# A small expert's rider on TensorE: partial sums kept in each column group, one transpose for each, and a written order

## The chip, the cores and the metric

One Trainium2 chip, one core. The metric is the device time of one execution in microseconds (us); of several executions the median is given. Instructions run on TensorE (PE, its weight loads listed apart as PEld), VectorE (DVE), ScalarE (ACT), GpSimd (POOL), and DMA queues that SyncE (SP) issues. Each engine has an instruction queue of its own.

## The reference

Three layers in a row, all in float32: attention with a learned relative bias, a mixture of experts, and a feed-forward layer. The change is in the second.

```python
x = attn_out.transpose(0, 2, 1, 3).reshape(1152, 512)
# mixture of experts: E = 8 experts, D = 512, F = 1024, capacity 288
logits = x @ w_gate
expert_idx = np.argmax(logits, axis=1)
gate_w = softmax(logits)[row, expert_idx]
# the first 288 rows of each expert, in order, are kept
h = np.maximum(np.einsum('ecd,edf->ecf', disp, w1), 0.0)
y = np.einsum('ecf,efd->ecd', h, w2)
out[i] = gate_w[i] * y[expert_idx[i], pos[i]]     # 0 for a row that is not kept
# feed-forward, 512 -> 2048 -> 512
h = x @ w_in
g = np.maximum(h, 0.0) + alpha * np.minimum(h, 0.0)
return g @ w_out
```

## The kernel before

Attention runs first. Routing then sorts the kept rows by expert into a table in DRAM, and the experts that got rows are worked off one after the other, each with its rows turned so that features lie on partitions. Matrices of the experts and of the last layer are split into a high and a low part (names ending in `h` and `l`), and each product is the sum of three products of parts. The course that runs in the traces (`J.mode == 1`) has a first expert of up to 288 rows (`job`, on `J.x`), a second one of up to 288 rows (`group(g1, ...)`, which calls `job` again), and a third one with at most 32 rows (`TINY`). Then `ffn(0, 608)` computes the last layer on the 608 rows of the table and sends each row to its place.

`job` goes over `f` = 0 to 7, slices of 128 of the expert's 1024 hidden units. `layer1(f)` (L690) is 12 matmuls of 128x128 weights on 288 columns into the tile `g`; ACT writes `hh = relu(g)`, DVE `hl`. `layer2(f - 1)` (L705) is 12 more into `acc`. The weights of two `f` come as one quarter of the expert (`raw`), which `raw_split` turns into `w1h, w1l, w2h, w2l` on ACT (L602) and DVE (L603). `side(2 * f)` is called between `layer1(f)` and `layer2(f - 1)`, `side(2 * f + 1)` behind the latter: at these 16 steps other work can be put in.

The third expert is such work, the **rider**. It holds few rows, so its weights are not split, and it computes in plain float32, which TensorE does in two passes for a matmul. The rows are the stationary operand (128x32), the weights stream, and four matmuls go to four groups of 32 columns of the array at once: matmul `c` writes partitions `32c` to `32c + 31` of the PSUM tile. `rider` gives back a `begin`, which loads the rows and the first matrix in quarters, and a list of steps; `RT` holds the number of the step at which each is called:

- `transpose` (L794): the 32 rows are turned to `x`, 4 chunks of 128 features (`xrT`, copied by DVE to `m`).
- `partial(q)` (L801), `q` = 0 to 3, a quarter of 256 hidden units each: the four column groups hold the four chunks of the contraction, 256 columns each; ACT copies the tile `part` to a `cell`.
- `hidden(q)` (L808): two matmuls with `fold`, a matrix of stacked identities, add the four chunks and turn the result, tile `hT`; ACT applies relu (L809) into `R.h`.
- `layer2(q)` (L818): the four column groups hold two chunks of the contraction by two halves of the 512 outputs, 256 columns each, added over `q` in `racc`.
- `finish`: ACT copies `racc`, two more matmuls with `fold` (`yT`, L826) add and turn, ACT and DVE write `yh` and `yl`, the input of the last layer.
- `load2(q)` (L777) loads a quarter of the second matrix over the quarter of the first one that `partial(q)` has read.

The parts of the first matrix lie in `AH["more"]` (named `ah` in the trace), in two halves of the quarter `raw` that `g1` has used up, and in two tiles `xj`.

Beside the rider the steps call `ahead(i)`, which converts the first 64-bit weights of the last layer (`d`, `cv`, `cw`; L860 on ACT, L862 to L864 on DVE). In the last layer `weights(f)` does the same for the other slices, from three buffers `d` that SP fills.

The part of the kernel up to the end of the first expert is under a manual schedule: on PE, ACT and DVE instructions stand in the order of the code. From `two_groups` on, a scheduler with a model of the costs orders each engine's instructions, SP's DMA issues too.

Of the kernel before, what the change touches and what calls it, by code (L numbers as in the profile page):

```python
# [15 lines left out]
AF = mybir.ActivationFunctionType  # L16
ALU = mybir.AluOpType
AX = mybir.AxisListType
ET = mybir.EngineType
# [13 lines left out]
BIG = float(1 << 20)  # L33
PRE0 = 10
NB = 2
RT = (0, 1, 2, 3, 4, 5, 6, 7, 9, 11, 12)
Q3 = 1
PRE = 4

# [1 line left out]
def build(tc, nc, a):  # L41
    V, A, G, T, SY = nc.vector, nc.scalar, nc.gpsimd, nc.tensor, nc.sync
    with contextlib.ExitStack() as ctx:
# [712 lines left out]
        def rider(g, e, yo):  # L756


            n = TINY
            w1, w2 = [a[z][ds(e, 1)].rearrange("a x y -> (a x) y") for z in ("ew1", "ew2")]  # L760
            x, xr = g.few[:, :, 0:n], g.ts[0][:n]
            R, S = Unit(), {}

            def cell():
                return M.p.tile([128, 512], F32, tag="cw", name="cell", bufs=4)

            def cells(q, n):

                t = [(AH["more"], *g1.t)[q]] if q < 3 else g.ts[1:]
                z = [z.rearrange("p (k c) -> p k c", c=n) for z in t]  # L770
                S[q] = [x[:, j] for x in z for j in range(x.shape[1])]
                return z

            def load(q, w, n):
                z = cells(q, n)
                for x, y in zip(z, (w,) if len(z) == 1 else (w[:, 0:512 // n], w[:, 512 // n:])):
                    SY.dma_start(x, y)  # L777

            def load1(q):
                load(q, w1[:, 256 * q:256 * q + 256].rearrange("(k p) c -> p k c", p=128), 256)  # L780

            def load2(q):
                load(q, w2[256 * q:256 * q + 256, :].rearrange("(f p) n -> p f n", p=128), 512)

            def begin():
                rows_of.other(SY.dma_start(xr, xd[ds(yo, n), 0:DM]))
                for q in range(4):
                    load1(q)

            def transpose():  # L790
                R.h = cell()
                ps = ps1(pt, "xrT")[:, 0:4 * n].rearrange("p (k n) -> p k n", k=4)
                for k in range(4):
                    T.transpose(ps[:, k], xr[:, 128 * k:128 * k + 128], ident[:n, :n])  # L794
                V.tensor_copy(x, ps)

            def partial(q):
                w = S[q]
                ps = ps1(pt, "part")[:, 0:256]
                for k in range(4):  # L800
                    T.matmul(ps[n * k:n * k + n], x[:, k], w[k], start=True, stop=True, skip_group_check=True)  # L801
                R.p = cell()[:, 0:256]
                A.copy(R.p, ps)

            def hidden(q):
                ps = ps1(pt, "hT")[:, 0:2 * n]
                for j in range(2):
                    T.matmul(ps[:, n * j:n * j + n], R.p[:, 128 * j:128 * j + 128], fold[:, 2 * n:3 * n], start=True, stop=True)  # L808
                A.activation(R.h[:, 2 * n * q:2 * n * q + 2 * n], ps, AF.Relu)  # L809

            def layer2(q):
                if q == 0:
                    R.acc = ps1(pt, "racc")[:, 0:256]
                w = S[q]
                for j in range(2):
                    for d in range(2):
                        o = n * (2 * j + d)
                        T.matmul(R.acc[o:o + n], R.h[:, n * (2 * q + j):][:, 0:n], w[j][:, 256 * d:256 * d + 256],  # L818
                                 start=q == 0, stop=q == 3, skip_group_check=True)

            def finish():
                y = cell()[:, 0:256]
                A.copy(y, R.acc)
                ps = ps1(pt, "yT")[:, 0:4 * n].rearrange("p (c r) -> p c r", c=2)
                for c in range(2):
                    T.matmul(ps[:, c], y[:, 128 * c:128 * c + 128], fold[:, 0:2 * n], start=True, stop=True)  # L826

                ps = ps.rearrange("p c (d r) -> p d c r", d=2)
                yh, yl = [z.rearrange("p (d c) r -> p d c r", d=2)[:, :, :, ds(yo, n)] for z in (M.yh, M.yl)]
                A.copy(yh, ps)  # L830
                V.tensor_tensor(yl, ps, yh.bitcast(F32), ALU.subtract)

            return begin, [(i, lambda f=f, q=q: f(*q)) for i, f, *q in (
                (RT[0], transpose), (RT[1], partial, 0), (RT[1], load2, 0),
                (RT[2], hidden, 0), (RT[2], partial, 1), (RT[2], load2, 1), (RT[3], hidden, 1), (RT[3], partial, 2), (RT[3], load2, 2),
                (RT[4], hidden, 2), (RT[4], partial, 3), (RT[4], load2, 3), (RT[5], hidden, 3), (RT[6], layer2, 0),
                (RT[7], layer2, 1), (RT[8], layer2, 2), (RT[9], layer2, 3), (RT[10], finish))]

        def to_dense(acc, yo, n):
            for d in range(2):  # L840
# [438 lines left out]

        def two_groups(g2, *more):  # L1280
            begin, todo = rider(g2, expert_of(2), row_of(2, [ET.SP, ET.Activation, ET.DVE]))
            group(g1, False, stepper(*more, *todo), begin)

        with tc.If(J.mode == 1) as course:  # L1284
            two_groups(prepare(2, 0), *[(2 * i + 1, lambda i=i: ahead(i)) for i in range(1, PRE)])
# [108 lines left out]
```

## Time and profile before

| | us |
|---|---|
| median of 3 executions | 357.55 |
| lowest, highest | 356.72, 361.35 |
| the profiled execution, its own time | 359.0 |
| span of the profile of that execution | 357.3 |
| PE busy in the span | 339.5 |
| second expert with the rider, first matmul to first matmul of the last layer | 35.55 |

The span runs from the first to the last instruction that the profiler saw; the execution's own time is 1.7 us longer, which lies around it. A row of the timeline is a run of like instructions on one engine: start, time from the first one's start to the last one's end, and what they write and read. Matmuls overlap on TensorE, so the time that a run takes up is read from its start to the start of the next row, not from its duration.

### The profile page before, as it was taken

How to read it: one execution, taken by the hardware profiler on the slowest of the kernel's cores; microseconds unless marked ns; L12 is line 12 of the kernel's file. 1: busy time of each engine (PE TensorE's matmuls, PEld its weight loads, DVE VectorE, ACT ScalarE, POOL GpSimd, SP SyncE). 2: the span in 40 equal slices, each digit the busy share in tenths (PEclk: the TensorE clock that was granted, in tenths of full speed). 3: DMA queues.
4: the chain of work that ended last, by engine and by line, in shares of the span. 5: the costliest groups of instructions: out<-in, count | busy, mean ns of one | idle time of the engine just before them, and what ended most of it. 6: DMA issues, size and time to landing. Idle time of an engine off the chain costs nothing. (4 is left out here: it accounts for less than half of the span.)

```text
span 357.3 us, 8970 instructions
## 1 busy us (share of the span) xinstructions
PE 339.5 (95%) x3372; PEld 273.2 (76%) x3373; DVE 278.7 (78%) x674; ACT 236.4 (66%) x585; POOL 58.8 (16%) x90
## 2 busy tenths in 40 slices
PE   4898999999999999999999999999999999999991
PEld 2334566677899788888899997799988988987880
DVE  4999989977788867876798795369999999988430
ACT  6959899987667675766774473357776656656430
POOL 2055333300000010462262100100000000000023
PEclk9999999999999999999999999999999999999997
DMA  7788969898999853948736996743546645530003
GB/s 301 223 257 273 333 244 354 313 285 313 339 411 337 276 206 108 332 154 258 222 71 189 361 288 187 246 150 125 178 119 189 190 152 178 175 120 3 0 29 118
DMA packets 42048, 76.90 MB, mean 215 GB/s; under 512 B 5159, under 2 KB 19623, under 8 KB 41996
## 3 DMA queue, kind: packets, MB, share of 16 engines
q1 hardware_dynamic: 40812, 73.76, 63.0%
q0 software_dynamic: 1184, 2.48, 1.9%
q8 instruction: 28, 0.46, 0.6%
q14 instruction: 24, 0.20, 0.2%
HBM read 57.53 MB, written 20.09 MB: 217 GB/s over the span
## 5 line engine op out<-in xcount | busy, mean ns | idle before, releaser
L273 ACT ACTIVATE p<-p,mn 128x576 f32<-128x576 f32 x72 | 55.6, 779 | 11.4 <-DVE mn L266 11.2
L259 PE MATMUL sps<-kqv 64*128 64x288 f32 x256 | 61.3, 427 | 0.3 <-DVE mn L266 0.2
L266 DVE CUSTOM_DVE_ANT_0 p<-sps,bias 128x576 f32<-128x576 f32 x72 | 52.4, 751 | 6.2 <-PE sps L252 3.6
L305 PE MATMUL t<-ident,p 64*128 64x64 f32 x640 | 52.6, 227 | 0.6 <-DVE PT L282 0.2
L183 DVE TENSOR_SCALAR h<-c 128x512 f32<-128x512 f32 (+17 forms) x121 | 49.5, 474 | 0.5 <-PE bps L192 0.4
L305 PEld LDWEIGHTS t<-ident,p 64*128 64x128 f32 x640 | 45.3, 139 | 6.0 <-ACT st L200 2.6
L280 ACT COPY PT<-t 128x320 f32<-128x320 f32 (+1 forms) x85 | 30.0, 404 | 24.7 <-PE sps L259 18.6
L259 PEld LDWEIGHTS sps<-kqv 64*128 64x128 f32 x256 | 37.2, 187 | 8.0 <-issue 4.1
L192 PE MATMUL bps<-h,c 128*32 128x512 f32 (+17 forms) x352 | 34.4, 489 | 8.0 <-DVE h L183 5.3
L323 PE MATMUL av<-PT,kqv 128*64 128x128 f32 x512 | 35.3, 279 | 0.8 <-ACT PT L280 0.3
L323 PEld LDWEIGHTS av<-PT,kqv 128*64 128x64 f32 x512 | 27.5, 137 | 8.6 <-ACT PT L280 4.1
L860 ACT ACTIVATE cv<-d 128x512 f32<-128x512 f32 x32 | 21.6, 676 | 14.8 <-DMA d<-in_win 5.5
L200 ACT ACTIVATE st<-bps,c 128x527 f32<-128x527 f32 (+35 forms) x72 | 30.6, 506 | 0.2 <-PE bps L192 0.2
L953 PE MATMUL facc<-w2h,hl 128*128 128x512 f32 (+1 forms) x75 | 29.9, 399 | 0.2 <-DVE hl L603 0.2
L953 PE MATMUL facc<-w2h,hh 128*128 128x512 f32 (+1 forms) x75 | 29.7, 396 | 0.0
L953 PE MATMUL facc<-w2l,hh 128*128 128x512 f32 (+1 forms) x75 | 29.6, 395 | 0.0
L192 PEld LDWEIGHTS bps<-h,c 128*32 128x32 f32 x352 | 10.6, 113 | 23.8 <-issue 7.4
L179 POOL TENSOR_SCALAR h<-c 128x448 f32<-128x448 f32 (+11 forms) x12 | 21.6, 1798 | 36.2 <-PE bps L192 19.5
L941 PE MATMUL fg<-yh,w1l 128*128 128x304 f32 x120 | 26.6, 303 | 0.0
L941 PE MATMUL fg<-yl,w1h 128*128 128x304 f32 x120 | 26.5, 302 | 0.0
L941 PE MATMUL fg<-yh,w1h 128*128 128x304 f32 x120 | 26.5, 302 | 0.0
L282 DVE COPY PT<-t 128x320 f32<-128x320 f32 (+1 forms) x43 | 18.8, 461 | 9.0 <-PE t L305 8.0
(232 smaller groups left out, 691.2 us busy)
## 6 DMA issues: line engine op xcount, KB each, us to landing
bias<-bd SPq DMA_DIRECT2D x23, 576.0 KB, 6.8
bd<-st SPq DMA_DIRECT2D x36, 295.5 KB, 6.7
raw<-in_ew SPq DMA_DIRECT2D x20, 512.0 KB, 6.5
d<-in_win SPq DMA_DIRECT2D x16, 512.0 KB, 3.8
d<-in_wout SPq DMA_DIRECT2D x16, 512.0 KB, 3.9
kqv<-in_kqva SPq DMA_DIRECT2D x6, 736.0 KB, 7.0
kqv<-in_kqvb SPq DMA_DIRECT2D x6, 672.0 KB, 9.3
xd<-zr SPq DMA_DIRECT2D x4, 722.8 KB, 8.6
```

The source lines that it names most:

```text
L179: G.tensor_scalar(h, tab[:, :n], psi[:, i:i + 1], 0.0, ALU.add, ALU.max)
L183: V.tensor_scalar(h, tab[:, :n], psi[:, i:i + 1], 0.0, ALU.add, ALU.max)
L192: T.matmul(ps[32 * c:32 * c + 32, n0:n1], w2n, hs[c][:, n0:n1], start=True, stop=True)
L200: A.activation(st[:, o:o + src.shape[1]], src, AF.Copy, scale=rr[:, t:t + 1])
L259: return [lambda n=n: T.matmul(ps[:, n, :288], q[u.ul][p], k[p, 288 * n:288 * n + 288], start=True, stop=True) for n in range(2)]
L266: V.tensor_tensor_reduce(out.rearrange("p (a b) -> p a b", a=2), ps[:, :, :288], bias.rearrange("p (a b) -> p a b", a=2), -0.125, 3.0e38, ...
L273: A.activation(out, out, AF.Exp, bias=mn, scale=-1.0, accum_out=acc)
L280: A.copy(o, i)
L305: return [lambda i=i, x=x: T.transpose(src[:, i], x[p], ident[p, p]) for i, x in enumerate(rows)], out
L323: T.matmul(o[p, c], u.v[:, j, p], rhs(h, j), start=j == 0, stop=False, skip_group_check=True)
L941: T.matmul(ps, w[:, 128 * k:128 * k + 128], x[:, k, s], start=k + i == 0, stop=k + i == 5)
L953: T.matmul(acc[i][:m], h[:, r:r + m], w, start=f == 0 and j == 0, stop=f == NF - 1 and j == 2)
```

## The change

`partial` now adds over the contraction: for a pair of quarters (`q` and `q + 1`) column group `c` holds 128 hidden units, and its four matmuls over `k` accumulate, so `part` is finished when it leaves PSUM and ACT applies relu at once. `hidden` turns it with one transpose. `layer2` and `finish` do the same with 128 outputs in each column group and the contraction over `f`. Called for `q` = 0 and 2 alone, that makes two `partial`, two `hidden`, two `layer2`. `RT` puts them at later steps, and TensorE is under the manual schedule within `group`.

```diff
-RT = (0, 1, 2, 3, 4, 5, 6, 7, 9, 11, 12)
+RT = (5, 8, 9, 10, 13, 14, 15)
...
             def partial(q):
-                w = S[q]
-                ps = ps1(pt, "part")[:, 0:256]
+                ps = ps1(pt, "part")[:, 0:128]
                 for k in range(4):
-                    T.matmul(ps[n * k:n * k + n], x[:, k], w[k], start=True, stop=True, skip_group_check=True)
-                R.p = cell()[:, 0:256]
-                A.copy(R.p, ps)
+                    for c in range(4):
+                        T.matmul(ps[n * c:n * c + n], x[:, k], S[q + c // 2][k][:, 128 * (c % 2):][:, 0:128], start=k == 0, stop=k == 3,
+                                 skip_group_check=True)
+                R.p = cell()[:, 0:128]
+                A.activation(R.p, ps, AF.Relu)
 
             def hidden(q):
-                ps = ps1(pt, "hT")[:, 0:2 * n]
-                for j in range(2):
-                    T.matmul(ps[:, n * j:n * j + n], R.p[:, 128 * j:128 * j + 128], fold[:, 2 * n:3 * n], start=True, stop=True)
-                A.activation(R.h[:, 2 * n * q:2 * n * q + 2 * n], ps, AF.Relu)
+                ps = ps1(pt, "hT")[:, 0:128]
+                T.transpose(ps, R.p, ident)
+                A.copy(R.h[:, 64 * q:64 * q + 128], ps)
 
             def layer2(q):
...
-                for j in range(2):
-                    for d in range(2):
-                        o = n * (2 * j + d)
-                        T.matmul(R.acc[o:o + n], R.h[:, n * (2 * q + j):][:, 0:n], w[j][:, 256 * d:256 * d + 256],
-                                 start=q == 0, stop=q == 3, skip_group_check=True)
+                for f in range(2 * q, 2 * q + 4):
+                    for c in range(4):
+                        T.matmul(R.acc[n * c:n * c + n], R.h[:, n * f:n * f + n], S[f // 2][f % 2][:, 128 * c:128 * c + 128],
+                                 start=f == 0, stop=f == 7, skip_group_check=True)
 
             def finish():
...
-                ps = ps1(pt, "yT")[:, 0:4 * n].rearrange("p (c r) -> p c r", c=2)
-                for c in range(2):
-                    T.matmul(ps[:, c], y[:, 128 * c:128 * c + 128], fold[:, 0:2 * n], start=True, stop=True)
...
+                ps = ps1(pt, "yT")[:, 0:128]
+                T.transpose(ps, y, ident)
...
-                (RT[0], transpose), (RT[1], partial, 0), (RT[1], load2, 0),
-                (RT[2], hidden, 0), (RT[2], partial, 1), (RT[2], load2, 1), (RT[3], hidden, 1), (RT[3], partial, 2), (RT[3], load2, 2),
-                (RT[4], hidden, 2), (RT[4], partial, 3), (RT[4], load2, 3), (RT[5], hidden, 3), (RT[6], layer2, 0),
-                (RT[7], layer2, 1), (RT[8], layer2, 2), (RT[9], layer2, 3), (RT[10], finish))]
+                (RT[1], partial, 0), (RT[1], load2, 0), (RT[1], load2, 1),
+                (RT[2], hidden, 0), (RT[2], partial, 2), (RT[2], load2, 2), (RT[2], load2, 3), (RT[3], hidden, 2),
+                (RT[4], layer2, 0), (RT[5], layer2, 2), (RT[6], finish))]
...
-            group(g1, False, stepper(*more, *todo), begin)
+            with tc.manual_schedule(engines={ET.PE}):
+                group(g1, False, stepper(*more, *todo), begin)
```

Line numbers behind the rider are four lower in the changed kernel (`fg` is L937 there, `facc` L949), and its `layer2` matmuls are L816.

On PE, around the rider's second layer, there stood before (a matmul's row names output tile, operands, output shape and count):

```order
L705 MATMUL acc<-hl,w2h 128x288
L818 MATMUL racc<-ah_3437,cell 32x256 x4
L705 MATMUL acc<-hl,w2h 128x288 x3
L690 MATMUL g_3893<-xh,w1h 128x288 x4
L690 MATMUL g_3893<-xl,w1h 128x288
L818 MATMUL racc<-raw_3393,cell 32x256 x4
L690 MATMUL g_3893<-xl,w1h 128x288 x3
L690 MATMUL g_3893<-xh,w1l 128x288 x4
L705 MATMUL acc<-hh,w2h 128x288
L818 MATMUL racc<-raw_3393,cell 32x256 x4
L705 MATMUL acc<-hh,w2h 128x288 x3
```

On PE at the same place of the changed kernel, behind `layer1(6)`:

```order
L690 MATMUL g_3911<-xh,w1l 128x288 x4
L705 MATMUL acc<-hh,w2h 128x288 x4
L705 MATMUL acc<-hh,w2l 128x288 x4
L705 MATMUL acc<-hl,w2h 128x288 x4
L816 MATMUL racc<-ah_3437,cell 32x128 x8
L816 MATMUL racc<-raw_3393,cell 32x128 x8
L690 MATMUL g_3957<-xh,w1h 128x288 x4
L690 MATMUL g_3957<-xl,w1h 128x288 x4
L690 MATMUL g_3957<-xh,w1l 128x288 x4
L816 MATMUL racc<-raw_3393,cell 32x128 x8
L816 MATMUL racc<-xj,cell 32x128 x8
L705 MATMUL acc<-hh,w2h 128x288 x4
```

The rider's matmuls, which stood in small groups within the runs of the second expert, now stand in groups of 16 between whole layers.

On DVE, from the start of the second expert, there stood before (`w1l` behind L603 is the low half of the second quarter's first matrix, L862 and L863 belong to `ahead`):

```order
L603 TENSOR_TENSOR w2l<-raw_3393,w2h 128x1024
L694 SCALAR_TENSOR_TENSOR hl<-g_3648,hh 128x288
L862 TENSOR_SCALAR ah_3437<-cv 128x512
L863 SCALAR_TENSOR_TENSOR ah_3437<-cv,ah_3437 128x512
L603 TENSOR_TENSOR w1l<-raw,w1h 128x1024
L694 SCALAR_TENSOR_TENSOR hl<-g_3688,hh 128x288
```

On DVE at the same place of the changed kernel:

```order
L603 TENSOR_TENSOR w2l<-raw_3393,w2h 128x1024
L694 SCALAR_TENSOR_TENSOR hl<-g_3650,hh 128x288
L858 TENSOR_SCALAR cw<-cv 128x512
L858 TENSOR_SCALAR ah_3437<-cv 128x512
L859 SCALAR_TENSOR_TENSOR cw<-cv,cw 128x512
L603 TENSOR_TENSOR w1l<-raw,w1h 128x1024
L694 SCALAR_TENSOR_TENSOR hl<-g_3675,hh 128x288
```

One more conversion (L858) now stands ahead of `w1l`. On SP the two DMAs of the expert's last quarter (L613, L615), which stood between the third and the fourth `load2`, now stand ahead of the first. On ACT the first conversion of the last layer's own weights (`cv<-d`, L856) has moved from behind `layer1(7)`'s `hh` and the rider's `yh` to between the rider's copy of `racc` and its `yh`.

## Rows read from the trace of the kernel before

**Rows 1.** The page: busy time, share of the span and instructions of TensorE.

```profile
PE 339.5 (95%) x3372; PEld 273.2 (76%) x3373; DVE 278.7 (78%) x674; ACT 236.4 (66%) x585; POOL 58.8 (16%) x90
```

**Rows 2.** Windows: stretch, its length, each engine's busy time, PE clock, DMA share, GB/s.

```profile
245.00:255.00 10.00, 10.00 (x57) 8.84 (x56) 10.00 (x21) 7.63 (x18) 0.00 (x0) 1.00 0.56 167
...
315.00:325.00 10.00, 9.77 (x51) 7.63 (x50) 8.41 (x17) 6.09 (x14) 0.00 (x0) 1.00 0.17 58
```

**Rows 3.** Timeline of PE: second expert's start, its third layer1, the last layer's start.

```profile
203.30 0.68 PE L690 MATMUL g<-xh,w1h 128*128 128x288 f32 x4
...
208.61 0.68 PE L690 MATMUL g<-xl,w1h 128*128 128x288 f32 x4
209.19 0.79 PE L690 MATMUL g<-xh,w1l 128*128 128x288 f32 x4
209.82 0.69 PE L705 MATMUL acc<-hh,w2h 128*128 128x288 f32 x4
...
238.85 1.39 PE L941 MATMUL fg<-yh,ah 128*128 128x304 f32 x8
```

**Rows 4.** Timeline of PE: the rider's first `partial` and `hidden` between matmuls of `acc`.

```profile
213.55 0.68 PE L705 MATMUL acc<-hh,w2h 128*128 128x288 f32 x4
214.16 0.64 PE L801 MATMUL part<-ah,m 128*32 128x256 f32 x8
214.73 0.79 PE L705 MATMUL acc<-hh,w2l 128*128 128x288 f32 x4
215.36 0.57 PE L808 MATMUL hT<-fold,cell 128*128 128x32 f32 x4
215.76 0.65 PE L705 MATMUL acc<-hl,w2h 128*128 128x288 f32 x3
216.34 0.64 PE L801 MATMUL part<-raw,m 128*32 128x256 f32 x8
```

**Rows 5.** Timeline of PE: the rider's `transpose`, and half of its last `layer2`.

```profile
211.93 0.29 PE L690 MATMUL g<-xl,w1h 128*128 128x288 f32 x1
212.15 0.43 PE L794 MATMUL xrT<-ident,xj 32*128 32x32 f32 x4
212.51 0.67 PE L690 MATMUL g<-xl,w1h 128*128 128x288 f32 x3
...
230.92 0.63 PE L818 MATMUL racc<-xj,cell 128*32 128x256 f32 x4
231.48 0.67 PE L690 MATMUL g<-xh,w1l 128*128 128x288 f32 x3
```

**Rows 6.** Timeline of PE in attention: a chain of accumulation in two column groups.

```profile
60.87 1.09 PE L323 MATMUL av<-PT,kqv 128*64 128x128 f32 x16
61.80 0.39 PE L325 MATMUL av<-PT,vd 128*64 128x128 f32 x4
```

**Rows 7.** Timeline of PE in routing: four column groups with 128 columns each.

```profile
168.90 0.43 PE L393 MATMUL lgT<-xT,c 128*32 128x128 f32 x8
169.26 1.30 PE L323 MATMUL av<-PT,kqv 128*64 128x128 f32 x15
```

**Rows 8.** Timeline of DVE at the start of the second expert.

```profile
206.85 0.42 DVE L862 TENSOR_SCALAR ah<-cv 128x512 int32<-128x512 int32 x1
207.30 0.69 DVE L863 SCALAR_TENSOR_TENSOR ah<-cv,ah 128x512 int32<-128x512 int32 x1
207.91 1.22 DVE L603 TENSOR_TENSOR w1l<-raw,w1h 128x1024 fp32r<-128x1024 f32 x1
```

**Rows 9.** ACT's and SP's timelines, and the DMAs of L777 from 198 to 262 us.

```profile
227.40 1.05 ACT L602 CAST w1h<-raw 128x1024 fp32r<-128x1024 f32 x1 [0.29 <-DMA raw<-in_ew]
...
219.81 0.37 SPq L613 DMA_DIRECT2D raw<-in_ew  x1
...
228.79 0.38 SPq L849 DMA_DIRECT2D d<-in_win  x1
...
DMA to landing us min/median/max: 3.6/6.8/8.4
```

More of the change, by code (lines that the diff above doesn't have):

```diff
@@ L811, in layer2 @@
+                A.copy(R.h[:, 64 * q:64 * q + 128], ps)
             def layer2(q):
                 if q == 0:
-                    R.acc = ps1(pt, "racc")[:, 0:256]
-                w = S[q]
-                for j in range(2):
-                    for d in range(2):
-                        o = n * (2 * j + d)
-                        T.matmul(R.acc[o:o + n], R.h[:, n * (2 * q + j):][:, 0:n], w[j][:, 256 * d:256 * d + 256],
-                                 start=q == 0, stop=q == 3, skip_group_check=True)
+                    R.acc = ps1(pt, "racc")[:, 0:128]
@@ L821, in finish @@
+                for f in range(2 * q, 2 * q + 4):
+                    for c in range(4):
+                        T.matmul(R.acc[n * c:n * c + n], R.h[:, n * f:n * f + n], S[f // 2][f % 2][:, 128 * c:128 * c + 128],
+                                 start=f == 0, stop=f == 7, skip_group_check=True)
             def finish():
-                y = cell()[:, 0:256]
+                y = cell()[:, 0:128]
                 A.copy(y, R.acc)
-                ps = ps1(pt, "yT")[:, 0:4 * n].rearrange("p (c r) -> p c r", c=2)
@@ L825, in finish @@
-                for c in range(2):
-                    T.matmul(ps[:, c], y[:, 128 * c:128 * c + 128], fold[:, 0:2 * n], start=True, stop=True)
-                ps = ps.rearrange("p c (d r) -> p d c r", d=2)
-                yh, yl = [z.rearrange("p (d c) r -> p d c r", d=2)[:, :, :, ds(yo, n)] for z in (M.yh, M.yl)]
+                ps = ps1(pt, "yT")[:, 0:128]
+                T.transpose(ps, y, ident)
+                ps = ps.rearrange("p (c r) -> p c r", c=4)
+                yh, yl = [z[:, :, ds(yo, n)] for z in (M.yh, M.yl)]
@@ L833, in rider @@
             return begin, [(i, lambda f=f, q=q: f(*q)) for i, f, *q in (
-                (RT[0], transpose), (RT[1], partial, 0), (RT[1], load2, 0),
-                (RT[2], hidden, 0), (RT[2], partial, 1), (RT[2], load2, 1), (RT[3], hidden, 1), (RT[3], partial, 2), (RT[3], load2, 2),
-                (RT[4], hidden, 2), (RT[4], partial, 3), (RT[4], load2, 3), (RT[5], hidden, 3), (RT[6], layer2, 0),
-                (RT[7], layer2, 1), (RT[8], layer2, 2), (RT[9], layer2, 3), (RT[10], finish))]
+                (RT[0], transpose), (RT[1], partial, 0), (RT[1], load2, 0), (RT[1], load2, 1),
+                (RT[2], hidden, 0), (RT[2], partial, 2), (RT[2], load2, 2), (RT[2], load2, 3), (RT[3], hidden, 2),
+                (RT[4], layer2, 0), (RT[5], layer2, 2), (RT[6], finish))]
         def to_dense(acc, yo, n):
```

## Prediction, made before the changed kernel was run

> **What bounds the kernel now.** I read the page's busy times first: TensorE is busy for 339.5 of 357.3 us [rows 1]. A share over the whole span says little about one stage, so the windows came next, over the second expert and the last layer: TensorE is busy for all of 245 to 255 us, at the full granted clock (1.00, the level of 2.4 GHz), and even in the worst stretch of the last layer, 315 to 325 us, for 9.77 of 10 us [rows 2]. So from 203 us to the end one thing sets the pace: the line of matmuls. A matmul taken out of it should bring the end forward by what it held of that line, if the other engines keep up. The timeline of PE, row by row, tells how much the rider holds.
>
> From the second expert's first matmul to the first one of the last layer are 35.55 us (at 203.30, 238.85) [rows 3]. The expert itself has 192 matmuls, 48 runs of four. The first ten runs take 203.30 to 208.61, 0.531 us each, so 48 take 25.5 us. 10.05 us are left. Of these 0.15 are a wait at 209 us, where two runs take 0.58 and 0.63 us in place of 0.53 (at 208.61, 209.19, 209.82) [rows 3], and about 0.1 stands in front of `fg`. **The rider holds 9.8 us** of the line.
>
> **The change part by part.** First, what it takes out, piece by piece, which must come to that figure. A `partial` takes 0.57 us from its own start to the next row's. But the run ahead of it takes 0.61 us and the run behind it 0.63, where a run alone takes 0.53: 0.08 to enter and 0.10 to leave (at 213.55, 214.16, 214.73, 215.36) [rows 4]. That is 0.75 us for a burst. `layer2` has the same shape, and its last call was cut in two by the scheduler; a half, with four passes in place of eight, takes 0.56 us, no less (at 230.92, 231.48) [rows 5]. So there are nine bursts, 6.75 us. A `hidden` takes 0.40 us and makes the three matmuls behind it, 0.40 alone, take 0.58, of which 0.08 are the next burst's entry: 0.49 us (at 215.36, 215.76, 216.34) [rows 4]. Four of them and the like pair in `finish` make 2.45. The `transpose` takes 0.36, 0.09 ahead of it and some 0.10 behind, 0.55 [rows 5]. The sum is 9.75 us, so the piece prices hold.
>
> What it puts there: the `transpose` stays, 0.55. Four new bursts, each a chain of eight passes of 128 columns in each of four column groups. No row shows that shape. The nearest is attention's `av`: a chain of eight passes of 128 columns in each of two column groups, accumulating in place as here, 0.93 us from start to next start [rows 6]. That four groups can run side by side at 128 columns, `lgT` shows: two passes in each of four groups in 0.36 us [rows 7], though without a chain. I take 0.93 plus 0.18 for entry and exit, 1.11 us a burst, 4.44 for four. From below the bound is 0.93, with no cost at the edges (0.7 us less in all). From above: if only two groups at a time went side by side, 1.86 + 0.18 = 2.04 a burst, 8.2 for four; if none did, 32 passes at 0.93 / 8 = 0.116, 3.9 with the edges, 15.6 for four. I take the first value, since it is the row with the chain and the other row shows the four groups.
>
> A rule speaks against splitting the streamed columns. The Trainium skill ("TensorEngine Tiling (Array Packing)", section "Instruction Overhead") says that each matmul carries some 60 cycles of overhead on trn2, and that no tiling factor should be taken from a dimension that is already small. Taken as an addition to each pass that would be an estimate of 0.025 us at 2.4 GHz, 0.2 us in a chain of eight, 0.8 for four bursts, and the gain below would be 2.7 us. The trace does not agree: eight passes of 128 columns, 1024 in a group, take 0.93 us [rows 6], and two passes of 256, 512 in a group, 0.57 [rows 4], so a column costs no more in the short passes.
>
> Three single transposes of 128 columns take the place of five pairs with `fold`. Four passes of `hidden` cost 0.49, so one costs between 0.12 (a quarter) and 0.49; with 0.11 for the pass and what remains of a `hidden` over its four passes (0.05) and its exit (0.08) it is 0.24, three 0.72. In all 0.55 + 4.44 + 0.72 = 5.7 us, and **4.05 us come out of the line**.
>
> **What is lost again.** The wait at 209 us is for `w1l`: DVE starts it at 207.91 with 1.22 us to go, and the matmuls that read it start at 209.19 [rows 3, 8]. In the changed order one more L858 stands ahead of it, 0.45 us by start to start (206.85 to 207.30), so TensorE waits 0.45 us longer at a place where it already waits: full price. The rest of this order is covered. Each `hidden` is ordered a whole layer (1.6 us) behind its `partial`, and ACT needs some 0.4 us for a relu of 128 columns. ACT's copy of the turned tile then holds up the casts of the last quarter, but `layer1(6)`, which needs them, is over 4 us away; the quarter itself is issued earlier, since SP no longer holds it behind three `load2` (219.81 before, and ACT waited for it at 227.40 [rows 9]); I count nothing for it, as TensorE did not wait for it before. `load2` waits for the two longer `partial`, about 218 and 221 us; `layer2` reads it at about 228 and 231, some 9 us later, and such loads took up to 8.4 us in a fuller queue [rows 9]. On ACT `cv<-d` now stands ahead of the rider's `yh` and of `yh` of the expert: if `d` landed as late as before (issued at 228.79, and loads took 3.6 us at the least [rows 9]) it would find ACT waiting since about 232, and `fg` would start up to 0.5 us late. I take 0.1, since the loads ahead of `d` in the queue lose 1 MB of traffic at that time. The gain is 4.05 - 0.45 - 0.1 = **3.5 us**: the expert's stretch goes from 35.55 to about 32 us, and the last layer runs as before, moved forward.
>
> **The rivals.** First, the groups do not run side by side when each is a chain. Then four bursts cost 15.6 us, the rider 16.9 in place of 9.75, and with the 0.45 the kernel is 7.6 us slower, 365.1. The point from which the sign turns is a burst of (9.75 - 0.55 - 0.72 - 0.55) / 4 = 2.0 us. Against it: eight passes of `lgT` in 0.36 us, 0.045 each, can only be side by side [rows 7]. With two at a time the time is 357.8. Second, VectorE takes the gain back. It is busy for 10.00 of 10 us at 245 to 255 [rows 2], converting weights for the last layer; if its work, and not TensorE's, set when the last slices are ready, half the gain or so would turn into waits in the last layer, 355.8. Against it: TensorE hardly waits for it now, and the conversions start behind `layer1(7)` and so move forward with TensorE. Third, the order written out waits where the scheduler's would not, for `load2`, or for ACT behind a late `d`: 1 to 2 us, 355.6. Fourth, edges and transposes cost little between whole layers, and the wait at 209 is not longer: 4.6 us, 352.9.
>
> **How the numbers follow.** The profiled execution took 359.0 us by its own time (357.3 of span), 1.45 above the median of 357.55; none of the terms lies in that difference, so the sum is taken from the one as from the other: 359.0 - 3.5 = 355.5 for an execution like that one, 357.55 - 3.5 = 354.05 for the median. Chances: the forecast 0.65, two groups at a time 0.05, none 0.05, VectorE 0.12, waits 0.07, the larger gain 0.06. The range of 8 in 10 goes from 352.6, past the larger gain, to 356.6, past the second and third rival with an execution's scatter; both cases of the first rival are left out. 2% of the time, about what a measurement of this kernel can tell from no change, are 7.15 us: a gain of that size would need the rider to cost almost nothing, 0.02; a loss of that size only the first rival's end gives, 0.04; within 2%, 0.94.
>
> **What would show it.** In the profile after: the four runs of `part` and `racc` of 32 passes at 0.93 us or near it, start to next start; a longer gap at `g<-xh,w1l` near 209 us, about 0.6 us over both runs in place of 0.15; the first `fg` near 235.3 us; the last layer as long as before, some 110 us to its last `facc`. The forecast is wrong if a burst takes 2 us, or if the last layer grows by what the expert lost, with TensorE waiting for `hl` or the weights of DVE.

## The result, and the profile after

| | before | after |
|---|---|---|
| median, us | 357.4 (6 executions) | 353.47 (6 executions) |
| lowest to highest, us | 356.5 to 361.35 | 352.35 to 355.37 |
| ratio, 95% interval | | 0.988, 0.9846 to 0.9915 |
| profiled execution, own time / span, us | 359.0 / 357.3 | 353.05 / 351.3 |

3.93 us between the medians, where 3.5 were forecast. "Stage" below is the time from the second expert's first `g` to the first `fg`, "last layer" from there to the start of the last `facc`. The page of the changed kernel, busy time of each engine, answers to [rows 1]:

```profile
PE 334.6 (95%) x3419; PEld 273.6 (78%) x3420; DVE 276.9 (79%) x674; ACT 235.1 (67%) x581; POOL 59.2 (17%) x90
```

TensorE is busy for 4.9 us less, and its share is still 95%. The span is 6.0 us shorter, so in this pair of profiles some waiting went too; a second profile of before (below) parts the two. TensorE has more instructions than before, 3419 for 3372, in less time. The windows of the last layer, as in [rows 2]:

```profile
245.00:255.00 10.00, 10.00 (x62) 9.21 (x62) 9.50 (x20) 7.00 (x16) 0.00 (x0) 1.00 0.50 159
315.00:325.00 10.00, 10.00 (x58) 8.90 (x57) 8.09 (x16) 6.42 (x17) 0.00 (x0) 1.00 0.00 1
```

TensorE stays full in both at a granted clock of 1.00, and VectorE (third figure after the length) now has half a microsecond to spare at 245 us. So the end still hangs on TensorE's line. The timeline of PE, as in [rows 3]: the expert's first matmuls, its third `layer1`, the first matmuls of the last layer, and the last `facc`:

```profile
202.51 0.68 PE L690 MATMUL g<-xh,w1h 128*128 128x288 f32 x4
...
207.82 0.68 PE L690 MATMUL g<-xl,w1h 128*128 128x288 f32 x4
208.60 0.79 PE L690 MATMUL g<-xh,w1l 128*128 128x288 f32 x4
209.23 0.69 PE L705 MATMUL acc<-hh,w2h 128*128 128x288 f32 x4
...
234.12 1.24 PE L937 MATMUL fg<-yh,ah 128*128 128x304 f32 x7
...
343.57 0.39 PE L949 MATMUL facc<-w2h,hl 128*96 128x512 f32 x1
```

The stage takes 234.12 - 202.51 = 31.61 us, 3.94 less than the 35.55 of [rows 3]; the last layer takes 109.45. In the profile of before it took 110.32, since TensorE waited there once; the experiments show whether that belongs to the change. At 208 us two runs take 0.78 and 0.63 us in place of 0.53 each: the wait for `w1l` grew from 0.15 to 0.35. One new burst and one new transpose in the same view, as in [rows 4, 5]:

```profile
215.60 0.69 PE L690 MATMUL g<-xh,w1l 128*128 128x288 f32 x4
216.22 0.30 PE L801 MATMUL part<-ah,m 128*32 128x128 f32 x2
...
217.03 0.28 PE L801 MATMUL part<-raw,m 128*32 128x128 f32 x2
217.24 0.80 PE L705 MATMUL acc<-hh,w2h 128*128 128x288 f32 x4
217.88 0.70 PE L705 MATMUL acc<-hh,w2l 128*128 128x288 f32 x4
...
221.85 0.27 PE L808 MATMUL hT<-ident,cell 128*128 128x128 f32 x1
221.88 0.77 PE L705 MATMUL acc<-hh,w2h 128*128 128x288 f32 x4
222.48 0.69 PE L705 MATMUL acc<-hh,w2l 128*128 128x288 f32 x4
```

The burst holds 1.02 us from its first row to the next `acc` (in the rows left out its 32 passes change between `ah` and `raw`, two passes at a time, from 216.22 on: the groups run side by side). The run ahead of it takes 0.62 and the run behind it 0.64 in place of 0.53, so it costs 1.02 + 0.09 + 0.11 = 1.22. The transpose is a single pass (x1), where a `hidden` was four; with 0.03 to the next start and 0.60 for the run behind it costs 0.10. The rider now holds 0.55 (`xrT`) + 4 x 1.22 + 3 x 0.10 = 5.7 us.

### The profile page after: what moved, and what is told of

It reads as the page before. It is cut to its first block, busy times and chain, and to the rows that moved or that the text cites. A ratio compares the mean times of both kernels' runs of the same rounds, so it can differ in the third digit from the quotient of the medians.

```text
span 351.3 us, 9056 instructions
## 1 busy us (share of the span) xinstructions
PE 334.6 (95%) x3419; PEld 273.6 (78%) x3420; DVE 276.9 (79%) x674; ACT 235.1 (67%) x581; POOL 59.2 (17%) x90
## 5 line engine op out<-in xcount | busy, mean ns | idle before, releaser
L259 PE MATMUL sps<-kqv 64*128 64x288 f32 x256 | 60.1, 426 | 0.0
L192 PE MATMUL bps<-h,c 128*32 128x512 f32 (+17 forms) x352 | 35.4, 496 | 7.4 <-DVE h L183 5.1
L856 ACT ACTIVATE cv<-d 128x512 f32<-128x512 f32 x32 | 21.7, 677 | 13.9 <-DMA d<-in_win 7.4
L192 PEld LDWEIGHTS bps<-h,c 128*32 128x32 f32 x352 | 11.4, 114 | 23.5 <-DVE h L183 7.6
L949 PE MATMUL facc<-w2h,hl 128*128 128x512 f32 (+1 forms) x75 | 29.7, 396 | 0.0
L949 PE MATMUL facc<-w2h,hh 128*128 128x512 f32 (+1 forms) x75 | 29.6, 395 | 0.0
L949 PE MATMUL facc<-w2l,hh 128*128 128x512 f32 (+1 forms) x75 | 29.6, 394 | 0.0
L179 POOL TENSOR_SCALAR h<-c 128x448 f32<-128x448 f32 (+11 forms) x12 | 22.4, 1864 | 34.7 <-PE bps L192 34.7
L937 PE MATMUL fg<-yh,w1l 128*128 128x304 f32 x120 | 26.6, 302 | 0.0
L937 PE MATMUL fg<-yl,w1h 128*128 128x304 f32 x120 | 26.5, 302 | 0.0
L937 PE MATMUL fg<-yh,w1h 128*128 128x304 f32 x120 | 26.5, 302 | 0.0
```

What stands on the lines that cost most here:

```text
L179: G.tensor_scalar(h, tab[:, :n], psi[:, i:i + 1], 0.0, ALU.add, ALU.max)
L192: T.matmul(ps[32 * c:32 * c + 32, n0:n1], w2n, hs[c][:, n0:n1], start=True, stop=True)
L259: return [lambda n=n: T.matmul(ps[:, n, :288], q[u.ul][p], k[p, 288 * n:288 * n + 288], start=True, stop=True) for n in range(2)]
L937: T.matmul(ps, w[:, 128 * k:128 * k + 128], x[:, k, s], start=k + i == 0, stop=k + i == 5)
L949: T.matmul(acc[i][:m], h[:, r:r + m], w, start=f == 0 and j == 0, stop=f == NF - 1 and j == 2)
```

## The experiments

Where a few tenths matter a median says little by itself: what precedes the stage differs by up to 1.7 us between profiles (it begins between 201.76 and 203.43 us). So each kernel has the stage and the last layer of its profile beside its time. All ratios are to the kernel before on the same chip.

| kernel | median us | ratio, 95% interval | stage us | last layer us |
|---|---|---|---|---|
| before, profiled again | 357.17 (one) | | 35.55 | 109.61 |
| after | 353.47 | 0.988, 0.9846 to 0.9915 | 31.61 | 109.45 |
| old sums, written order | 356.18 | 0.997, 0.9955 to 0.9985 | 34.59 | 109.47 |
| new sums, scheduled | 352.79 | 0.9888, 0.9864 to 0.9912 | 31.60 | 109.47 |
| group after group | 358.35 | 1.0041, 1.0021 to 1.0062 | 37.14 | 109.45 |
| pairs of groups | 356.03 (one) | | 33.45 | 109.46 |
| no rider | 348.92 | 0.9769, 0.9745 to 0.9794 | 26.73 | 110.68 |
| joined bursts, one part tile | 351.77 (one) | | 30.93 | 109.45 |
| the same, no wait | 351.59 | 0.9847, 0.9827 to 0.9868 | 30.70 | 109.47 |
| joined bursts, two tiles | 352.66 | 0.9877, 0.9858 to 0.9895 | 30.93 | 109.45 |
| the same, no wait | 351.88 | 0.9862, 0.9832 to 0.9892 | 30.73 | 109.46 |
| after, again | 352.56 | 0.9867, 0.9843 to 0.9890 | 31.60 | 109.46 |
| two tiles, no wait, again | 351.79 | 0.9854, 0.9828 to 0.9879 | 30.71 | 109.46 |

**Old sums, written order.** The kernel before with one call of the rider at each step from 5 on, and TensorE's order written out: the order's share by itself.

```diff
-RT = (0, 1, 2, 3, 4, 5, 6, 7, 9, 11, 12)
+RT = (5, 6, 7, 8, 9, 10, 11, 12, 13, 14, 15)
-            group(g1, False, stepper(*more, *todo), begin)
+            with tc.manual_schedule(engines={ET.PE}):
+                group(g1, False, stepper(*more, *todo), begin)
```

> The rider's old arithmetic (contraction split over the column groups, folds), with TensorE's order written out and the rider's eleven steps at 5 to 15. Theory: the arithmetic makes the gain, since it halves the bursts and takes out the folds. Then the rider holds eight bursts of 0.75, five folds of 0.49 and the transpose's 0.55, 9.0 us, and the second expert goes from 35.55 to some 34.9 us; the time is 356.7 (0.6 to 0.8 less than before, most of it the burst that the scheduler had cut in two). Rival: the written order makes the gain, since nothing is put inside a layer any more. Then the expert takes some 32 us and the time is near the changed kernel's 353.5.

The timeline of PE of this kernel, the stage's two ends, the wait for `w1l`, and one `partial` of the old form between whole layers:

```profile
201.87 0.68 PE L690 MATMUL g<-xh,w1h 128*128 128x288 f32 x4
...
207.17 0.68 PE L690 MATMUL g<-xl,w1h 128*128 128x288 f32 x4
207.95 0.79 PE L690 MATMUL g<-xh,w1l 128*128 128x288 f32 x4
...
212.43 0.64 PE L801 MATMUL part<-ah,m 128*32 128x256 f32 x8
212.99 0.79 PE L705 MATMUL acc<-hh,w2h 128*128 128x288 f32 x4
213.62 0.69 PE L705 MATMUL acc<-hh,w2l 128*128 128x288 f32 x4
...
236.46 0.83 PE L941 MATMUL fg<-yh,ah 128*128 128x304 f32 x4
```

34.59 us: 0.96 less than before (34.9 was expected), although a burst costs no less here (0.56 and 0.10 on the run behind it). What it no longer has is the ninth burst, the `layer2` that the scheduler had cut in two, 0.75. The wait for `w1l` works the other way: it is 0.35 us here too (0.78 and, to 208.58, 0.63), 0.20 more than before. So the rider itself went from 9.8 us to 34.59 - 25.5 - 0.35 - 0.1 = 8.6. Of the 1.2 us by which it fell the ninth burst is 0.75, and about 0.3 comes from three `hidden` that now stand right ahead of a `partial`: one pair takes 1.13 us (214.69 to 215.71, and 0.11 on the run behind) where the prices of before add up to 0.49 + 0.75. The other 2.98 us of the stage's 3.94, from 34.59 to 31.61, are the arithmetic's, with the same wait in both kernels: three quarters.

**New sums, scheduled.** The changed kernel without the written order.

```diff
-            with tc.manual_schedule(engines={ET.PE}):
-                group(g1, False, stepper(*more, *todo), begin)
+            group(g1, False, stepper(*more, *todo), begin)
```

> The new arithmetic and its steps, with TensorE's order left to the scheduler, which now puts every burst between whole layers too and cuts only one layer for the transpose. Theory: 353.5, within 0.5 us of the changed kernel, and an expert of 31.6 us within 0.3. Rival: the written order has a share of its own of 1 us or more, and the time is 354.5 or above.

The timeline of PE of this kernel, the stage's two ends:

```profile
203.02 0.69 PE L690 MATMUL g<-xh,w1h 128*128 128x288 f32 x4
...
234.62 1.39 PE L937 MATMUL fg<-yh,ah 128*128 128x304 f32 x8
```

The stage takes 31.60 us, the changed kernel's own figure. With the new sums at the new steps the written order is worth nothing; the 0.96 us of the first experiment came with old calls that were many and could be cut, or with their steps, which these two runs don't part. They do place the longer wait for `w1l`: it is 0.35 us here as well (208.33, 209.10, 209.74), without the written order, and in the first experiment without the new sums. What both share with the changed kernel, and not with before, is that the rider's first step is number 5 and not 0.

**Group after group.** The four column groups of a burst one after the other, the same 32 passes.

```diff
-                for k in range(4):
-                    for c in range(4):
+                for c in range(4):
+                    for k in range(4):
...
-                for f in range(2 * q, 2 * q + 4):
-                    for c in range(4):
+                for c in range(4):
+                    for f in range(2 * q, 2 * q + 4):
```

> The changed kernel with the two loops of partial and of layer2 exchanged: all the matmuls of one column group, then those of the next. The sums are the same. Theory: matmuls start in order, so the four chains can only overlap where they are issued in turn; here each chain waits for the one ahead, 32 passes at 0.11 us, some 3.7 us a burst with its edges in place of 1.2, and the kernel is 10 us slower than the changed one, near 363.4. Rival: the groups overlap in whatever order they are issued; then the time stays at 353.5.

The timeline of PE of this kernel; groups 0 and 1 read `ah`, groups 2 and 3 `raw`:

```profile
216.47 1.20 PE L801 MATMUL part<-ah,m 128*32 128x128 f32 x13
217.40 0.30 PE L801 MATMUL part<-raw,m 128*32 128x128 f32 x1
...
218.86 0.80 PE L705 MATMUL acc<-hh,w2h 128*128 128x288 f32 x4
```

The loss is there, but not at its forecast size: a burst takes 2.39 us (216.47 to 218.86), not 3.7. The third group starts 0.93 us after the first, so each starts some 0.47 after the one ahead, half of a chain of eight passes (0.93 for eight, 0.116 each): at its fifth pass. The 13 passes ahead of it fit, eight of group 0 and five of group 1. The rows between show it too, `raw` and `ah` in turn from 217.40 to 217.75. My theory of no overlap fell; groups issued one after the other overlap by half a chain here. The stage follows: 31.61 + 4 x (2.39 - 1.02) = 37.1, measured 37.14.

**Pairs of groups.** A test of that reading: groups 0 and 1 in turn, then 2 and 3.

```diff
-                for k in range(4):
-                    for c in range(4):
+                for c0 in (0, 2):
+                    for k in range(4):
+                        for c in (c0, c0 + 1):
```

and the same in `layer2`.

> The changed kernel with the rider's matmuls issued for column groups 0 and 1 in turn, and then for groups 2 and 3 in turn. With one group after the other a chain started 0.467 us behind the one ahead, at its fifth pass of eight, so TensorE seems to look about four matmuls ahead. Theory: the second pair starts when three or four of the first pair's sixteen passes are left, some 0.7 us after the first, and a burst takes 0.7 + 0.9 = 1.6 us: an expert of 33.8 us. Rivals: no look-ahead across pairs, 1.75 us a burst and 34.5; any look-ahead that reaches 16 matmuls, 1.02 a burst and 31.6.

The timeline of PE of this kernel:

```profile
217.15 0.74 PE L802 MATMUL part<-ah,m 128*32 128x128 f32 x10
217.63 0.30 PE L802 MATMUL part<-raw,m 128*32 128x128 f32 x2
...
218.62 0.80 PE L705 MATMUL acc<-hh,w2h 128*128 128x288 f32 x4
```

The second pair starts 0.48 us after the first, at the row for the first pair's tenth pass of sixteen, and the burst takes 1.47 us. That the next pair comes half a chain later again, and not a whole one, bears out the overlap by half a chain: 31.61 + 4 x 0.45 = 33.4, measured 33.45. The reason that the expectation gave for it failed: with a look-ahead of about four matmuls over all groups the second pair would have waited 0.7 us, and a burst would have taken 1.6. The tenth pass of sixteen is the fifth of each group, as in the order before. So in both orders the next groups start with a chain's fifth pass of eight. What sets that point the runs don't tell.

**No rider.** Steps of the rider left out: the third expert is not computed and its weights are not loaded, so its rows are missing from the last layer's input.

```diff
-                group(g1, False, stepper(*more, *todo), begin)
+                group(g1, False, stepper(*more))
```

> The changed kernel without the rider: the third expert is not computed, nor are its weights loaded, and its rows stay zero. Theory: TensorE's line sets the time, so what the rider still holds (5.7 us) comes off the end: an expert of some 25.9 us, a last layer of 109.5 us as in the changed kernel, 347.8 us. Rival: VectorE, over 90% busy in the last layer, sets its pace once TensorE comes earlier; then the last layer grows by 1 us or more, with TensorE waiting for hl or for weights, and the time is 349 or above.

The timeline of PE of this kernel, the rows with an idle time before them (in brackets, with what ended it):

```profile
229.02 1.39 PE L937 MATMUL fg<-yh,ah 128*128 128x304 f32 x8 [0.68 <-ACT yh L839]
...
296.17 0.55 PE L937 MATMUL fg<-yh,w1h 128*128 128x304 f32 x2 [0.32 <-ACT g L940]
...
313.99 0.50 PE L949 MATMUL facc<-w2h,hl 128*128 128x512 f32 x1 [0.30 <-DVE hl L603]
```

This bounds what a cheaper rider can still give. The time falls by 4.5 us (353.47 to 348.92), not by the whole 5.7 that the rider holds, and ends between the theory's 347.8 and the rival's 349. The stage gives 4.88, since TensorE waits for ACT's `yh` in front of `fg`; the last layer takes 110.68 us in this profile, 1.23 more, with waits for ACT and VectorE. How much of the 1.23 is the kernel's is open: the profiled execution, 349.71 us, is the slowest of four and 0.8 over their median, and one of the two waits, for `hl` some 85 us into the last layer, stands where the first profile of before had its own (below). Waits of the kind that the prediction's second rival names do come, then, but deeper: not where the changed kernel is, nor where the joined versions below are (109.45).

**Before, profiled again.** To see what of the last layer's 0.87 us belongs to the change.

> The kernel before, profiled once more, since its last layer took 110.32 us in the one profile and 109.45 in three profiles of the changed kernel and its variants. If that 0.9 us belongs to the order of its instructions, the last layer takes 110.2 to 110.4 again, with TensorE waiting for hl near 322 us; if it was the scatter of one execution, 109.5. The expert takes 35.55 in either case.

The timeline of PE of this kernel, then its window of 315 to 325 us (the row beside [rows 2]):

```profile
202.30 0.69 PE L690 MATMUL g<-xh,w1h 128*128 128x288 f32 x4
...
237.85 1.38 PE L941 MATMUL fg<-yh,ah 128*128 128x304 f32 x8
...
347.46 0.39 PE L953 MATMUL facc<-w2h,hl 128*96 128x512 f32 x1
```

```profile
315.00:325.00 10.00, 10.00 (x58) 8.64 (x57) 8.53 (x16) 6.24 (x16) 0.00 (x0) 1.00 0.13 48
```

The wait in the first profile of before, by its timeline of PE (the matmul ahead of this one starts at 322.86):

```profile
323.48 0.51 PE L953 MATMUL facc<-w2h,hl 128*128 128x512 f32 x1 [0.23 <-DVE hl L603]
```

The stage is 35.55 us again; the last layer takes 109.61, and TensorE is full where it had 9.77. So 0.7 of the 0.87 us were that execution's. The other 0.16 may be the change's: 0.14 of it stands at the same slice in this profile too (two matmuls from 321.50 to 322.10, 0.60 us in place of 0.46), and nothing does in the changed kernel. The spans compare at 355.4 and 351.3, 4.1 us, of which the stage is 3.94; by the two pages TensorE is busy for 338.7 and 334.6 us, 4.1 us less as well, so what went was work.

**Joined bursts.** The two `partial` stand together, the two `hidden`, and the two `layer2`, so TensorE enters and leaves the column groups twice, not four times.

```diff
-RT = (5, 8, 9, 10, 13, 14, 15)
+RT = (5, 8, 9, 10, 14, 14, 15)
...
-                (RT[0], transpose), (RT[1], partial, 0), (RT[1], load2, 0), (RT[1], load2, 1),
-                (RT[2], hidden, 0), (RT[2], partial, 2), (RT[2], load2, 2), (RT[2], load2, 3), (RT[3], hidden, 2),
+                (RT[0], transpose), (RT[1], partial, 0), (RT[1], partial, 2), (RT[1], load2, 0), (RT[1], load2, 1),
+                (RT[1], load2, 2), (RT[1], load2, 3), (RT[2], hidden, 0), (RT[2], hidden, 2),
```

In this first form the two calls share the name of the part tile, so both `hidden` turn the second part, and the third expert's sums use the second half of its hidden units twice; the instructions and their number are those of the whole computation.

> The changed kernel with the bursts joined alone, the wait at 209 us left. Theory: an expert of 31.2 us, 0.4 less than the changed kernel's, the wait of 0.35 us still there. Rival: longer chains cost more than their passes, and the expert is not shorter.

With it ran a form in which VectorE's first conversions for the last layer (L858) are ordered behind `w1l`, so that TensorE needn't wait at 208 us (`after` is the instruction that writes `w1l`):

```diff
-        def f64_convert(t, w):
+        def f64_convert(t, w, after=None):
...
-            V.tensor_scalar(w, v, 3, 0x7FFFFFF8, ALU.logical_shift_left, ALU.bitwise_and)
+            i = V.tensor_scalar(w, v, 3, 0x7FFFFFF8, ALU.logical_shift_left, ALU.bitwise_and)
+            if after is not None:
+                behind(i, after)
```

> The changed kernel with both calls of partial, both of hidden and both of layer2 put next to each other, which makes two bursts of 64 passes out of four of 32, and with VectorE's conversions for the last layer ordered behind the w1l that TensorE waited for at 209 us. Theory: what a burst costs beyond its passes is the entry and exit, 0.2 us, so 0.4 us go, and the wait of 0.35 us goes: an expert of 30.9 us in place of 31.6, a time 0.7 us below the changed kernel (352.5 to 352.9). Rival: bringing TensorE forward uses up the slack of ScalarE and VectorE at the start of the last layer and the 0.7 us turn into waits there; then the expert is as short, the last layer longer than 109.5 us, and the time that of the changed kernel.

Stage 30.93 and 30.70 us, less than the 31.2 and 30.9 expected: joining saves more than the 0.2 us of a burst's edges, as the rows below show (the second form's time, 351.59 us, is under the expected 352.5 too). Both again with a part tile for each `hidden`:

```diff
-                R.p = cell()[:, 0:128]
-                A.activation(R.p, ps, AF.Relu)
+                R.p[q] = cell()[:, 0:128]
+                A.activation(R.p[q], ps, AF.Relu)
```

> The changed kernel with both partial calls in one place and both hidden calls in one place, each part kept in a tile of its own, so that TensorE enters and leaves column groups three times and not four. Theory (a burst costs the line of matmuls its passes at 0.87 us and about 0.35 us for entry, first pass and exit, the latter once for a joined pair): the joined pair takes 1.88 us for two of 1.02 plus edges; the stage about 30.9 us in place of 31.6; the time about 0.6 us under that of the changed kernel, 352.6 to 352.9. Rival (the stage is not what sets the end any more, since VectorE converts the weights of the last layer): the last layer grows by what the stage lost, to 110.0 us and more, and the time stays near 353.4.

> The kernel of e10 with the conversions for the last layer ordered on VectorE behind the subtraction that makes w1l, the low half of the expert's second quarter. Theory (the wait for w1l at 209 us is at full price): the two runs of matmuls there take 1.06 us in place of 1.41; a wait of some 0.1 us comes up at the next quarter (about 214.5 us) where the conversions then stand; the stage about 30.7 us, the time 0.2 us under e10, some 352.4. Rival (VectorE's conversions, put later, make the last layer start or run later): the stage is shorter by 0.2, the last layer longer by as much, and the time equal to e10.

The timeline of PE of the first of these two, the joined `partial` and the joined transposes (two passes in a row):

```profile
216.12 0.30 PE L801 MATMUL part<-ah,m 128*32 128x128 f32 x2
...
218.00 0.80 PE L705 MATMUL acc<-hh,w2h 128*128 128x288 f32 x4
...
219.71 0.38 PE L808 MATMUL hT<-ident,cell 128*128 128x128 f32 x2
219.84 0.78 PE L690 MATMUL g<-xh,w1h 128*128 128x288 f32 x4
220.46 0.69 PE L690 MATMUL g<-xl,w1h 128*128 128x288 f32 x4
```

A joined pair takes 1.88 us. The second chain thus adds 0.86, and of a burst's 1.22 us 0.36 are the price of being a burst of its own. Two pairs are joined (two entries, where the expectation says three), so 0.7 us should go: 31.61 - 0.7 = 30.9, measured 30.93, with the last layer at 109.45 as before. The ratio, 0.9877, can't be told from the changed kernel's; the stage tells it.

The form without the wait, timeline of PE at the second and at the third quarter's `w1l`:

```profile
207.80 0.68 PE L690 MATMUL g<-xl,w1h 128*128 128x288 f32 x4
208.32 0.68 PE L690 MATMUL g<-xh,w1l 128*128 128x288 f32 x4
208.84 0.69 PE L705 MATMUL acc<-hh,w2h 128*128 128x288 f32 x4
...
214.67 0.69 PE L690 MATMUL g<-xl,w1h 128*128 128x288 f32 x4
215.27 0.80 PE L690 MATMUL g<-xh,w1l 128*128 128x288 f32 x4
216.00 0.30 PE L801 MATMUL part<-ah,m 128*32 128x128 f32 x2
```

and its timeline of DVE:

```profile
206.87 1.23 DVE L603 TENSOR_TENSOR w1l<-raw,w1h 128x1024 fp32r<-128x1024 f32 x1 [0.74 <-ACT w1h L602]
...
214.00 1.22 DVE L603 TENSOR_TENSOR w1l<-raw,w1h 128x1024 fp32r<-128x1024 f32 x1
```

The wait of 0.35 us is gone at 208 us (0.52 and 0.52), since `w1l` starts as soon as ACT has `w1h`, and the conversions stand behind it (from 208.38 on). But the conversions now delay the third quarter's `w1l` to 214.00, and TensorE waits there: 0.60 and 0.73 us, where the joined form took 0.53 and 0.62. Of 0.35 us 0.2 stay: stage 30.73.

**On one chip.** The changed kernel and the last version once more, unedited.

> The changed kernel once more, unedited, for a comparison on one chip with the joined version. Theory (the last layer of the first profile of before, 110.32 us, held 0.7 us of scatter, and the gain is what the stage lost): stage 31.6 us, last layer 109.45 us again, ratio to the kernel before 0.988 to 0.989, which is 4.0 us. Rival (the changed order makes the last layer shorter too): the last layer varies with the run and the ratio comes nearer to 0.985.

> The kernel of e11 once more, unedited, beside the changed kernel. Theory: stage 30.7 us, last layer 109.45 us, 0.9 us under the changed kernel on the same chip. Rival (what the stage saves of VectorE's order is paid elsewhere): within 0.3 us of the changed kernel.

Stages 31.60 and 30.71 us, last layers 109.46 both: 0.89 us apart, as expected. The medians are 352.56 and 351.79, 0.77 apart, but the executions overlap (352.11 to 352.83, and 351.22 to 353.44) and so do the intervals of the two ratios. The changed kernel's ratio, 0.9867, lies between what the two views expected; its last layer, the same to 0.01 us as in the first profile, speaks for the first. The joined version is the fastest one here by every profile; the times by themselves don't settle 0.8 us.

## Why the prediction held

**The line of TensorE, taken as the bound,** was right: the stage gave 3.94 us, and the median went by 3.93. That the two agree to 0.01 is chance: the interval of the ratio reaches from 3.0 to 5.5 us, and the changed kernel's second measurement has 4.4 between the medians. TensorE is full up to the end at the full granted clock, in the second profile of before as in the changed kernel, so what leaves the line leaves the time. Where 0.68 or 0.9 us more came out (joined bursts), the last layer kept its length again.

**The burst** was the term with the widest bounds, 0.93 to 3.9 us, and the value taken from `av`, 1.11, came out at 1.22. The 0.93 of [rows 6] ends where a row of the same kind follows. Ahead of a whole layer the last pass holds 0.21 us to the next run (217.03 to 217.24), where passes in the burst are 0.11 apart; the prediction took its burst without that. The joined pair shows it: a further chain of eight costs 0.86, the rest, 0.36, is paid once a burst. I had 0.18 for it, from bursts of two passes a group.

**The three transposes** were mis-sized the other way: 0.10 each and not 0.24. I took 0.11 for the pass, which was right, and added 0.13 for the rest of a `hidden` and its exit, which was paid already. A row of before, the old `finish`, could have told (timeline of PE):

```profile
233.54 0.55 PE L826 MATMUL yT<-fold,cell 128*128 128x64 f32 x4
233.90 0.76 PE L690 MATMUL g<-xh,w1h 128*128 128x288 f32 x4
234.51 0.69 PE L690 MATMUL g<-xl,w1h 128*128 128x288 f32 x4
```

Four passes between whole layers cost 0.36 and 0.08 on the run behind, 0.44: 0.11 a pass with the exit in it. The two errors, +0.44 and -0.42, cancel, and 5.7 us for the rider was right by that luck.

**The wait for `w1l`** did move the way the changed order says, at the price that TensorE waits in full, but by 0.20 and not by 0.45. The first two experiments, taken together, put it down to the later steps. The VectorE rows:

```profile
206.05 0.42 DVE L858 TENSOR_SCALAR cw<-cv 128x512 int32<-128x512 int32 x1
206.38 0.42 DVE L858 TENSOR_SCALAR ah<-cv 128x512 int32<-128x512 int32 x1
206.72 0.69 DVE L859 SCALAR_TENSOR_TENSOR cw<-cv,cw 128x512 int32<-128x512 int32 x1
207.32 1.22 DVE L603 TENSOR_TENSOR w1l<-raw,w1h 128x1024 fp32r<-128x1024 f32 x1
```

From the first L858 to `w1l` are 1.27 us, 1.06 in [rows 8]. The second L858 doesn't read what the first one writes and starts 0.33 behind it, and it also stands between the first one and its reader, which before stood 0.45 behind. Here an instruction put between two that depend on each other cost 0.21 us, less than its own step. Taking the wait away (0.35 us at 208 us) gave 0.2 net, since the next quarter then waits.

**The start of `fg`** lost nothing: 0.38 us from the last `acc` run to `fg` in the second profile of before, 0.37 after; I had counted 0.1. By the measured terms the sum is 9.75 - 5.7 - 0.2 = 3.85 us, and the stage shows 3.94.

**The rivals.** Groups that don't run side by side: they do when the code takes them in turn, and the price of the other order is shown, not argued: 2.39 us a burst and a slower kernel (1.0041, 1.0021 to 1.0062), on the slow side of the break-even of 2.0 us that the prediction gave. VectorE taking the gain back: no wait for it in the changed kernel's last layer; with 4.9 us more out of the stage up to 1.23 us come back in the one profile, for ACT as much as for VectorE. Waits of the written order: none, the scheduler's own order gives 31.60 as well. The larger gain of 4.6 us needed edges that cost little and no longer wait; the transposes bear it out, the bursts and the wait don't. The Trainium skill's rule of overhead for each matmul ("TensorEngine Tiling (Array Packing)", section "Instruction Overhead"), added to every pass of a chain, would have made the gain 2.7 us; a further chain of eight costs 0.86 us in a joined burst, less than the 0.93 of [rows 6], so nothing comes on top of the rows' price here. What part of the rows' own price is overhead the runs don't tell, nor does the prediction's comparison (0.93 us for 1024 columns, 0.57 for 512), since the 0.57 holds what a burst costs beside its passes.

The written order and the new steps are the part that stays partly open: with the old sums they bring 0.96 us together, and which of the two does it was not tried. In the rider's own line they are 1.2 us, of which the longer wait takes 0.2 back.

## What to carry to other kernels

Where one engine is full to the end, price an edit by start-to-start times of its rows, with the rows on either side, and check it on the stage rather than on the median: 0.2 us show there, where executions scatter by more than 1 us. Column groups pay when the code takes them in turn, and each stay in them has an entry and an exit, so few long stays beat many short ones; whatever partial sums can be kept in PSUM save a pass to add them. An instruction that joins an engine's queue ahead of something waited for costs what it delays that thing by, which was less than its own length here, where it filled the gap between two dependent ones, and moving it away put the delay on the next one in the queue.

## What the runs showed of the hardware

- Chains of eight passes of 128 columns in four column groups: in turn 1.02 us for all 32 passes; one group after the other 2.39 us, each group's first pass some 0.47 us behind that of the group ahead, half a chain; two groups in turn and then the other two, 1.47 us. I had expected no overlap at all there (3.7 us).
- A burst in column groups between layers that use the whole array costs 0.36 us beside its passes (1.22 alone, 0.86 for a further chain in a joined burst), 0.20 of them in the runs ahead of it and behind it.
- One float32 transpose of a 128x128 tile between whole layers takes 0.10 us of TensorE's line; two in a row 0.13 us to the next start, and 0.22 with the run behind them: some 0.11 a pass, as for the four passes of the old `yT` (0.44).
- VectorE starts a 128x512 int32 operation 0.33 us behind an independent one of its kind, and 0.45 us behind one whose output it reads.
